# A fused attention and mixture-of-experts kernel: a rebuilt opening, spread activation loads, two weight low halves on VectorE and a moved routing step

## The chip, the core and the metric

The kernel runs on one core of a Trainium2 chip. That core has TensorE (matrix products into PSUM), VectorE, ScalarE and GpSimd (element work), SyncE (here a queue that issues transfers) and 16 DMA engines. The metric is the device time of one execution in microseconds (us), lower is better. In the views PE is TensorE, DVE is VectorE, ACT is ScalarE, POOL is GpSimd and SP is SyncE.

## The reference

```python
def _attn_ref(q, k, v, g_norm):            # (4, 8, 576, 64) each
    kv = np.einsum('bhsd,bhse->bhde', k, v)
    out = np.einsum('bhsd,bhde->bhse', q, kv)
    rms = np.sqrt(np.mean(out * out, axis=-1, keepdims=True) + 1e-06)
    return (out / rms * g_norm)
def _moe_ref(x, w_gate, w1, w2):           # N=2304, D=512, E=8, F=1024
    P = np.exp(logits - logits.max())      # logits = x @ w_gate
    for _ in range(8):
        P /= P.sum(1, keepdims=True) + 1e-09
        P /= P.sum(0, keepdims=True) + 1e-09
        P *= N / E
    for e in range(E):                     # every token through every expert
        out += P[:, e:e + 1] * (np.maximum(x @ w1[e], 0.0) @ w2[e])
def _moe2_ref(x, expert_emb, tau, w1, w2): # each token through one expert
    logits = xn @ en.T / tau               # xn, en: rows divided by their norms
    expert_idx = np.argmax(logits, axis=1)
    gate_w = softmax(logits)[np.arange(N), expert_idx]
    for e in range(E):
        mask = expert_idx == e
        out[mask] = gate_w[mask, None] * (np.maximum(x[mask] @ w1[e], 0.0) @ w2[e])
```

The last stage's output is the result: attention, then the first mixture, then the second.

## The kernel before

All products are fp32 made of two fp32r parts. A weight or an activation is split into a high half (a cast) and a low half (the rest, `raw - high`), and each product is three matmuls: high by high, high by low, low by high. The split of one 512 KB weight quarter is one `prep(g)`: ScalarE casts the high half `wh` (L158), and the low half `wl` is made either by VectorE in one instruction over 128x1024 (L165, L257) or by GpSimd in two over 128x512 (L163).

The first mixture walks 3 blocks of 768 tokens by 8 experts (step s = 8·block + expert). Its up product uses seven combined products n = 0 to 6 instead of eight (`fill`, L1018): each pairs a combination of weight quarters with one of the activation quarters x11, x21, t2, t3, t4, t1, x22. An activation combination has its own high and low parts, made by `x_split`; for instance `ready_t2` forms `x12-x11` and t2 on VectorE. Each product n has eight columns of work i = 0 to 7 in two loops; `ahead(g)` prepares the weight combination three products ahead (`prep` where it has to be split, `fetch` from a stored copy `w1c`, `w2c` in later blocks), and in the first step (s=0) the table `opening` gives the pieces of attention that are put behind each column. Blocks 1 and 2 have the activations of their four quarters loaded from `xd` by `x_stage` (L300); the down product there is `down` (L1154), whose stored weights `w2c` come on the same SyncE queue.

The opening runs attention for batches 0 to 3, in chunks c = 0 to 4 of up to 128 rows. `att_kv(b, chunks)` accumulates kᵀv (L411), `att_out` multiplies by q (L422), `squares`, `norm_b`, `norm_c` and `scale_rows` (L425 to L439) normalise, `turn` (L446, L447) transposes rows into x. The first `fill` needs x11, which chunks 0 to 2 of batch 0 hold, and the split of w11 (`prep(0)`). Batch 0 comes first, and the others are put between `fill`s.

Element work without a due time is kept in lists (`hooks`: gates, Sinkhorn rows) that advance one entry for each column of the up product in steps s=1 and on; `thooks` are the quarter combinations on GpSimd in that stage.

The second mixture runs each token through one expert: tokens are counted and sorted by matmuls with one-hot matrices (L861 with `B` and `G`), gathered by row by GpSimd's indirect transfers (L1590), and go in blocks of 256 through `f1` (up, L644, then `hh` = relu on ScalarE L648 and `hl` = low half on VectorE L649) and `f2` (down, L664). The gate weight of a token is found from `gate_parts` (L852 to L855): a chain of eight VectorE instructions, three times cast to bf16 and multiply (612 elements a lane), with two subtractions; here called through `q_parts`. Two dynamic blocks follow the fixed ones. The last part goes by blocks of 128 tokens through `single` (L1609 on), where relu gives `hrow`, a transpose on TensorE `hth` and its low half `htl` (L1633).

Of the kernel before, what the change touches and what calls it, by code (L numbers as in the profile page):

```python
# [18 lines left out]
P = 128  # L19
# [25 lines left out]
def tile_linattn_moe_moe(ctx: ExitStack, tc: tile.TileContext, qT, k, v, g2, wg, w1a, w2a, emb, embT, tau, w1b, w2b, out):  # L45
# [246 lines left out]
    def x_stage(blk):  # L292
# [5 lines left out]
        for i, t in enumerate(ts):  # L298
            c = o + i % 2 * HB
            nc.sync.dma_start(t, xd[:, i // 2 * 2:i // 2 * 2 + 2, c:c + HB])  # L300
        return ts
# [235 lines left out]
    for c in range(NSC - 1):  # L537
        load_kv(1, c)
    load_quarter(0, "w11", raws[0, "w11"])
    load_kv(1, NSC - 1)  # L540
# [4 lines left out]
    for c in range(3):  # L545
        load_kv(2, c)
    for name in ("w21", "w22"):
        load_quarter(0, name, raws[0, name])
    for c in range(3, NSC):
        load_kv(2, c)  # L550
    outs = []
    for c in range(NSC):
# [3 lines left out]
        squares(ps, n, c, (junk, x2t)[c % 2])  # L556
        outs.append(ps)
    norm_b(slice(0, NSC))
    norm_c(slice(0, NSC))
    prep(0, nc.gpsimd)  # L560
    for c in range(NSC):
        scale_rows(xs0[c], outs[c], rows_of(c), c)
    att_kv(1, range(NSC - 1))
    for c in range(NSC - 1):
        load_kv(3, c)
# [6 lines left out]
    for c in range(3):  # L572
        first_turn(c)
    for kk in range(2):
        nc.scalar.copy(x_part(0, 0)[:, kk], x11[:, kk])  # L575
        nc.vector.tensor_tensor(x_part(0, 1)[:, kk], x11[:, kk], f32(x_part(0, 0)[:, kk]), ALU.subtract)
    att_kv(1, (NSC - 1,))
# [29 lines left out]
    def open_first():  # L607
# [4 lines left out]
        0: [first_pieces, lambda: att_kv(2, (0,)), lambda: gate_logits(0, 0, 3)],  # L612
        1: [lambda: first_turn(3), lambda: att_kv(2, (1,)), lambda: gate_logits(0, 1, 3)],
        2: [lambda: first_turn(4), lambda: load_kv(3, 4), lambda: stream_turn(1, 0), lambda: gate_logits(0, 2, 3),
            lambda: att_kv(2, (2,)), lambda: prep(2)],
        3: [lambda: stream_turn(1, 1), ready_t2, lambda: att_kv(2, (3, 4)), open_first],
        4: [lambda: x_split("t2", t2), lambda: ahead(0), lambda: gate_logits(3, 3, 6)],
        5: [ready_t3, lambda: gate_logits(3, 4, 6)],
        6: [lambda: gate_logits(3, 5, 6)],
        7: [lambda: att_kv(3, (0,)), lambda: stream_load_q(1)],  # L620
# [403 lines left out]
    def ahead(g):  # L1024
        h = g + 3
        if h < len(seq_of):
            s, n = seq_of[h]
            if s < E or h in plain_at or n >= 7 and not quick(s):
                pool = n in POOL_LOW and (s, n) != (NSTEP - 1, 9) if s < E or not quick(s) and n >= 7 else True
# [199 lines left out]
    n_att = 12  # L1229
# [17 lines left out]
    hooks.extend([sk_max, rest, sk_max1, rest, rest, sk_exp, rest, rest])  # L1247
# [8 lines left out]
    for s in range(NBK * E):  # L1256
# [39 lines left out]
        for n in range(7):  # L1296
# [5 lines left out]
            for i in range(4):  # L1302
# [43 lines left out]
                if i == 1 and g > 0:  # L1346
                    ahead(g)
                if s == 0:
                    for f in opening.get(4 * n + i, ()):
                        f()  # L1350
                if (n, i) in xup:
# [13 lines left out]
        if e == E - 1 and blk + 1 < NBK and not fast:  # L1365
            xq = x_steps(*x_stage(blk + 1))
# [519 lines left out]
```

## Time and profile before

| what | value |
|---|---|
| median of 3 runs | 1792.01 us (1791.96 to 1793.23) |
| the profiled execution, its own time | 1792.93 us |
| span of the trace | 1791.1 us |
| TensorE busy | 1766.2 us (99%), 11494 matmul records |
| VectorE, ScalarE, GpSimd busy | 1244.5 (69%), 849.8 (47%), 1044.6 (58%) us |
| mean granted TensorE clock | 0.998 |

The profiled execution is 0.92 us above the median. The span leaves 1.8 us of its time outside the trace. TensorE is nearly always busy, so the time is the sum of its matmuls, of the time before the first and after the last of them, and of its waits between.

### The profile page before, as it was taken

The page shows a single profiled execution, that of the slowest core. Times are in us where ns is not written, and L with a number is a line of the kernel's source. Part 1 is how long each engine was busy: PE and PEld are TensorE (multiplying, and loading weights), DVE is VectorE, ACT ScalarE, POOL GpSimd, SP SyncE. Part 2 cuts the span into 40 slices and gives each one's busy share as a digit, 9 for nine tenths or more (in the row PEclk, how much of TensorE's full clock was granted, in tenths as well). Part 3 has the DMA queues.
Part 4 walks back from the last instruction along what each step waited for, and adds up shares of the span by engine and source line. Part 5 has one row for each costly group of instructions (what it writes and reads, how often), then busy time and mean ns, then how long its engine had stood idle before and what let it go on. Part 6 is the DMA issues. An engine that isn't in the chain of part 4 may idle for free. (4 is left out here: it accounts for less than half of the span.)

```text
span 1791.1 us, 30992 instructions
## 1 busy us (share of the span) xinstructions
PE 1766.2 (99%) x11494; PEld 1677.6 (94%) x11494; DVE 1244.5 (69%) x2184; ACT 849.8 (47%) x1444; POOL 1044.6 (58%) x867
## 2 busy tenths in 40 slices
PE   7999999999999999999999999999999999999997
PEld 7989889989998999999999999999999998888996
DVE  5946686566657788876456769897567763877665
ACT  4645345444434634544444553554454433556553
POOL 3403379889879655774467566765477432554222
PEclk9999999999999999999999999999999999999999
DMA  9626458779868765556566666566465653588664
GB/s 313 229 59 210 142 207 298 257 262 334 287 232 279 278 221 209 200 190 230 173 222 221 213 228 239 184 218 224 168 214 187 232 203 108 188 315 290 230 232 147
DMA packets 183585, 397.22 MB, mean 222 GB/s; under 512 B 16384, under 2 KB 84480, under 8 KB 183168
## 3 DMA queue, kind: packets, MB, share of 16 engines
q1 hardware_dynamic: 177200, 377.15, 61.2%
q0 software_dynamic: 3840, 12.59, 2.0%
q10 hardware_dynamic: 2384, 5.41, 0.9%
q8 instruction: 92, 1.51, 0.3%
q14 instruction: 69, 0.57, 0.1%
HBM read 314.08 MB, written 81.00 MB: 221 GB/s over the span
## 5 line engine op out<-in xcount | busy, mean ns | idle before, releaser
L1018 PE MATMUL A<-xo,wh 128*128 128x384 f32 x2688 | 689.0, 338 | 0.5 <-ACT xo L575 0.2
L1018 PEld LDWEIGHTS A<-xo,wh 128*128 128x128 f32 x2688 | 482.1, 188 | 3.0 <-DVE u L1006 0.8
L1018 PE MATMUL A<-xo,wl 128*128 128x384 f32 x1344 | 452.1, 336 | 1.4 <-POOL wl L163 1.4
L1154 PE MATMUL A<-wh,d 128*128 128x256 f32 x2520 | 432.2, 276 | 0.2 <-DMA wh<-w2c 0.2
L163 POOL TENSOR_TENSOR wl<-raw,wh 128x512 fp32r<-128x512 f32 x180 | 246.7, 1392 | 289.3 <-ACT wh L158 134.8
L1154 PEld LDWEIGHTS A<-wh,d 128*128 128x128 f32 x2520 | 381.0, 188 | 0.4 <-issue 0.4
L1154 PE MATMUL A<-wl,d 128*128 128x256 f32 x1260 | 348.0, 276 | 0.8 <-DMA wl<-w2c 0.8
L1018 PEld LDWEIGHTS A<-xo,wl 128*128 128x128 f32 x1344 | 252.6, 188 | 2.6 <-POOL wl L163 2.6
L1387 PE MATMUL A<-wh,d 128*128 128x512 f32 x768 | 243.8, 392 | 0.0
L1154 PEld LDWEIGHTS A<-wl,d 128*128 128x128 f32 x1260 | 236.5, 188 | 1.0 <-DMA wl<-w2c 1.0
L1003 DVE SCALAR_TENSOR_TENSOR d<-A,d 128x384 fp32r<-128x384 f32 x228 | 125.9, 553 | 153.7 <-ACT raw L1313 84.1
L163 POOL TENSOR_TENSOR wl<-rb,wh 128x512 fp32r<-128x512 f32 x92 | 129.3, 1426 | 158.6 <-ACT wh L158 158.6
L1387 PEld LDWEIGHTS A<-wh,d 128*128 128x128 f32 x768 | 144.2, 188 | 29.8 <-issue 0.3
L1008 ACT ACTIVATE d<-A 128x384 fp32r<-128x384 f32 x132 | 65.5, 497 | 196.8 <-DVE A L1006 193.8
L1387 PE MATMUL A<-wl,d 128*128 128x512 f32 x384 | 149.5, 389 | 0.0
L1309 ACT COPY qs<-A 128x384 f32<-128x384 f32 x96 | 45.6, 479 | 178.8 <-PE A L1018 175.5
L158 ACT CAST wh<-raw 128x1024 fp32r<-128x1024 f32 x94 | 98.5, 1048 | 14.6 <-DMA raw<-in_w1a_dram 7.3
L257 DVE TENSOR_TENSOR wl<-raw,wh 128x1024 fp32r<-128x1024 f32 x45 | 70.7, 1573 | 35.3 <-ACT wh L256 25.4
L1387 PEld LDWEIGHTS A<-wl,d 128*128 128x128 f32 x384 | 72.2, 188 | 14.0
L1006 DVE TENSOR_TENSOR A<-A,qs 128x384 f32<-128x384 f32 x132 | 73.6, 560 | 16.2 <-PE A L1018 15.9
L158 ACT CAST wh<-rb 128x1024 fp32r<-128x1024 f32 x46 | 48.6, 1056 | 59.8 <-DMA rb<-in_w1a_dram 27.4
L1209 POOL TENSOR_TENSOR d<-qs,d 128x384 fp32r<-128x384 f32 x60 | 66.8, 1143 | 16.9 <-ACT d L1207 16.9
(524 smaller groups left out, 3399.8 us busy)
## 6 DMA issues: line engine op xcount, KB each, us to landing
raw<-in_w1a_dram SPq DMA_DIRECT2D x64, 512.0 KB, 4.7
wh<-w1c SPq DMA_DIRECT2D x64, 512.0 KB, 5.0
wl<-w1c SPq DMA_DIRECT2D x64, 512.0 KB, 6.0
wh<-w2c SPq DMA_DIRECT2D x60, 512.0 KB, 5.3
wl<-w2c SPq DMA_DIRECT2D x60, 512.0 KB, 6.1
raw<-in_w2a_dram SPq DMA_DIRECT2D x51, 512.0 KB, 4.3
raw<-in_w1b_dram SPq DMA_DIRECT2D x48, 512.0 KB, 6.4
raw<-in_w2b_dram SPq DMA_DIRECT2D x48, 512.0 KB, 4.1
```

Source lines behind the costliest of these rows:

```text
L158: nc.scalar.copy(hi, raw)
L163: eng.tensor_tensor(lo[:, c], raw[:, c], f32(hi[:, c]), ALU.subtract)
L257: after_two.append([2, lambda: nc.vector.tensor_tensor(lo, src, f32(hi), ALU.subtract)])
L1003: nc.vector.scalar_tensor_tensor(hl[:, i, :], src, 0.0, f32(hh[:, i, :]), ALU.max, ALU.subtract)
L1006: nc.vector.tensor_tensor(dst, ps, u, ALU.add)
L1008: nc.scalar.activation(hq[a][0][:, i, :], dst, AF.Relu)
L1018: nc.tensor.matmul(ps[:, 0:HB], a[:, fs], bb[:, kk, :], start=(first and j == 0), stop=(j == 5), skip_group_check=True)
L1154: nc.tensor.matmul(o, a[:, f, ts_], bb[:, ds_], start=(m in first and j != 1 and i == 0), stop=(i == 11), skip_group_check=True)
L1209: nc.gpsimd.tensor_tensor(a12[1][:, i], qs[:, i], f32(a12[0][:, i]), ALU.subtract)
L1309: nc.scalar.copy(qs[:, i, :], p)
L1387: nc.tensor.matmul(ys[j], a, bb[:, ds_], start=(m + ff + i == 0), stop=(m == 3 and ff == 1 and i == 2))
```

## The change

It has five parts.

- **Opening.** The load of w11 goes ahead of batch 1's chunks on the SyncE queue, those of batch 2 ahead of w21 and w22. The normalisation of batch 0 is cut into chunks 0 to 2 (`first_norm`, `first_scale`) and 3 to 4, and `prep(0)` stands after the first part. Batch 1's kᵀv is taken in three pieces, with the turns of chunks 0 to 2 between them and the last two chunks behind columns of s=0. The table `opening` is in another order: `ready_t2`, `ready_t3` and their splits stand ahead of `ahead(0)` and `ahead(1)`, which move two columns back, and the low half of `prep(2)` is made by GpSimd instead of VectorE. The entries of `hooks` begin two columns later.
- **Two low halves.** For product 6 of steps 3 and 7 VectorE makes `wl` instead of GpSimd.
- **Activation loads.** The four loads of block 2's activations, 384 KB each, are issued at columns 3 of products 0, 2, 4, 6 of the last expert but one, instead of together after product 6.
- **Routing.** `q_idx` and the first gather stand one `f1` slot later; `q_parts` moves from column 4 of the last fixed `f2` to slot 3 of the first dynamic block's `f1`; one Sinkhorn entry moves by one.
- **Single blocks.** In `single` one weight split (`split_w2(1)`) stands after the first transpose, and the low half of the next block's first W1 quarter after the second.

```diff
@@ x_stage
-        for i, t in enumerate(ts):
+
+        def load(i, t):
             c = o + i % 2 * HB
             nc.sync.dma_start(t, xd[:, i // 2 * 2:i // 2 * 2 + 2, c:c + HB])
-        return ts
+
+        return ts, [lambda i=i, t=t: load(i, t) for i, t in enumerate(ts)]
@@ opening
-    for c in range(NSC - 1):
+    load_quarter(0, "w11", raws[0, "w11"])
+    for c in range(NSC):
         load_kv(1, c)
-    load_quarter(0, "w11", raws[0, "w11"])
-    load_kv(1, NSC - 1)
...
+    def first_norm(c0, c1):
+        for c in range(c0, c1):
+            squares(outs[c], rows_of(c), c, (junk, x2t)[c % 2])
+        norm_b(slice(c0, c1))
+        norm_c(slice(c0, c1))
+
+    def first_scale(c0, c1):
+        for c in range(c0, c1):
+            scale_rows(xs0[c], outs[c], rows_of(c), c)
+
...
-        squares(ps, n, c, (junk, x2t)[c % 2])
         outs.append(ps)
-    norm_b(slice(0, NSC))
-    norm_c(slice(0, NSC))
+    first_norm(0, 3)
     prep(0, nc.gpsimd)
-    for c in range(NSC):
-        scale_rows(xs0[c], outs[c], rows_of(c), c)
-    att_kv(1, range(NSC - 1))
+    first_scale(0, 3)
+    att_kv(1, range(2))
...
     for c in range(3):
         first_turn(c)
+    att_kv(1, (2,))
...
-    att_kv(1, (NSC - 1,))
+    first_norm(3, NSC)
+    first_scale(3, NSC)
...
     opening = {
-        0: [first_pieces, lambda: att_kv(2, (0,)), lambda: gate_logits(0, 0, 3)],
-        1: [lambda: first_turn(3), lambda: att_kv(2, (1,)), lambda: gate_logits(0, 1, 3)],
-        2: [lambda: first_turn(4), lambda: load_kv(3, 4), lambda: stream_turn(1, 0), lambda: gate_logits(0, 2, 3),
-            lambda: att_kv(2, (2,)), lambda: prep(2)],
-        3: [lambda: stream_turn(1, 1), ready_t2, lambda: att_kv(2, (3, 4)), open_first],
-        4: [lambda: x_split("t2", t2), lambda: ahead(0), lambda: gate_logits(3, 3, 6)],
-        5: [ready_t3, lambda: gate_logits(3, 4, 6)],
-        6: [lambda: gate_logits(3, 5, 6)],
-        7: [lambda: att_kv(3, (0,)), lambda: stream_load_q(1)],
+        0: [lambda: att_kv(1, (3,))],
+        1: [lambda: att_kv(1, (4,))],
+        2: [first_pieces, lambda: gate_logits(0, 0, 3), lambda: gate_logits(0, 1, 3)],
+        3: [lambda: att_kv(2, (0,)), lambda: gate_logits(0, 2, 3), lambda: att_kv(2, (1,)), lambda: first_turn(3),
+            lambda: first_turn(4), lambda: load_kv(3, 4), lambda: att_kv(2, (2,)), lambda: att_kv(2, (3, 4)),
+            open_first, lambda: prep(2, nc.gpsimd)],
+        4: [lambda: stream_turn(1, 0), lambda: stream_turn(1, 1), ready_t2],
+        5: [lambda: x_split("t2", t2), lambda: gate_logits(3, 3, 6)],
+        6: [ready_t3, lambda: gate_logits(3, 4, 6), lambda: gate_logits(3, 5, 6), lambda: ahead(0)],
+        7: [lambda: ahead(1), lambda: att_kv(3, (0,)), lambda: stream_load_q(1)],
@@ ahead
-                pool = n in POOL_LOW and (s, n) != (NSTEP - 1, 9) if s < E or not quick(s) and n >= 7 else True
+                pool = n in POOL_LOW and (s, n) not in ((NSTEP - 1, 9), (3, 6), (7, 6)) if s < E or not quick(s) and n >= 7 else True
@@ hooks
-    hooks.extend([sk_max, rest, sk_max1, rest, rest, sk_exp, rest, rest])
+    hooks[:0] = [rest] * 2
+    hooks.extend([sk_max, rest, sk_max1, rest, sk_exp, rest])
@@ steps of the first mixture
+                if fast and e == E - 2 and blk + 1 < NBK and i == 3 and n % 2 == 0:
+                    if n == 0:
+                        staged, staging = x_stage(blk + 1)
+                    staging.pop(0)()
...
         if fast:
-            if e == E - 2 and blk + 1 < NBK:
-                staged = x_stage(blk + 1)
             down(s, blk, e)
@@ single
         split_w2(0)
-        split_w2(1)
         t0 = relu(p0)
         up(p1, 1, 0, 6)
         turn(t0)
+        split_w2(1)
         split_w2(2)
...
-        split_w1(0)
+        low0 = split_w1(0)
         turn(t1)
+        low0()
@@ routing
-        if f == 5:
+        if f == 6:
             q_idx()
             gather(0)
...
-        if f == 4:
-            q_parts()
...
             def slot(f):
                 if f % 2 == 0:
                     split_w2(f // 2)
+                if n == 0 and f == 3:
+                    q_parts()
```

The lines below are each engine's instructions in program order, with the line numbers of the kernel they belong to (those of the changed kernel are some ten to twenty higher).

VectorE at the first dynamic block, before (L852 to L855 is `q_parts`, L649 makes an `hl` for each of the eight columns of `f1`, L165 a weight's low half):

```order
L852 CAST gp_16204<-gr_16203 128x18
L853 TENSOR_TENSOR G_15645<-A_15643,gp_16204 128x18x34
L1602 TENSOR_SCALAR y<-A,iota_i 128x512
L649 SCALAR_TENSOR_TENSOR hl_15670<-A,hh_15669 128x256
L165 TENSOR_TENSOR g3l<-raw_15711,g3h 128x1024
L649 SCALAR_TENSOR_TENSOR hl_15698<-A,hh_15697 128x256
L649 SCALAR_TENSOR_TENSOR hl_15732<-A,hh_15731 128x256
L649 SCALAR_TENSOR_TENSOR hl_15752<-A,hh_15751 128x256
L649 SCALAR_TENSOR_TENSOR hl_15778<-A,hh_15777 128x256
L165 TENSOR_TENSOR g1l<-raw_15713,g1h 128x1024
```

and in the changed kernel:

```order
L165 TENSOR_TENSOR g3l<-raw_15715,g3h 128x1024
L659 SCALAR_TENSOR_TENSOR hl_15702<-A,hh_15701 128x256
L659 SCALAR_TENSOR_TENSOR hl_15736<-A,hh_15735 128x256
L659 SCALAR_TENSOR_TENSOR hl_15756<-A,hh_15755 128x256
L862 CAST gp_16305<-gs 128x18
L863 TENSOR_TENSOR G_15649<-A_15647,gp_16305 128x18x34
L865 TENSOR_TENSOR gr_16304<-gs,gp_16305 128x18
L862 CAST gp_16305<-gr_16304 128x18
L863 TENSOR_TENSOR G_15649<-A_15647,gp_16305 128x18x34
L865 TENSOR_TENSOR gr_16304<-gr_16304,gp_16305 128x18
L862 CAST gp_16305<-gr_16304 128x18
L863 TENSOR_TENSOR G_15649<-A_15647,gp_16305 128x18x34
```

The chain of `q_parts` stood ahead of the block's `hl`s, and now stands behind the fourth of them; the next rows of the changed kernel are the fifth `hl` and `g1l`.

TensorE in the opening, before (L411 is kᵀv, L446 a turn, L1018 the first product of the mixture; `qs`, `u`, `kv` hold batch 1's chunks):

```order
L411 MATMUL A<-qs 128x128 x4
L411 MATMUL A<-u_153,qs 128x128 x4
L411 MATMUL A<-u_153 128x128 x4
L411 MATMUL A<-kv 128x128 x4
L446 MATMUL M<-ident,xs_148 128x128 x12
L411 MATMUL A<-kv 128x128 x4
L1018 MATMUL A<-xo,wh 128x384 x2
L1018 MATMUL A<-xo,wl 128x384
L1018 MATMUL A<-xo,wh 128x384 x2
L1018 MATMUL A<-xo,wl 128x384
L422 MATMUL M<-ax,q_147 64x128 x4
L422 MATMUL M<-ax,q_147 128x128 x4
```

and in the changed kernel, where L413, L448 and L1028 are the same three:

```order
L413 MATMUL A<-qs 128x128 x4
L413 MATMUL A<-u_153,qs 128x128 x4
L448 MATMUL M<-ident,xs_148 128x128 x12
L413 MATMUL A<-u_153 128x128 x4
L1028 MATMUL A<-xo,wh 128x384 x2
L1028 MATMUL A<-xo,wl 128x384
L1028 MATMUL A<-xo,wh 128x384 x2
L1028 MATMUL A<-xo,wl 128x384
L413 MATMUL A<-kv 128x128 x4
L1028 MATMUL A<-xo,wh 128x384 x2
L1028 MATMUL A<-xo,wl 128x384
L1028 MATMUL A<-xo,wh 128x384 x2
```

The turns of batch 0 stand two chunks of batch 1 earlier, and its last two chunks stand behind the first columns of the product.

GpSimd in the opening, before (L163 is a low half, L263 a weight combination, L290 an activation's low half):

```order
L290 TENSOR_TENSOR xo<-x_145,xo 128x384 x2
L163 TENSOR_TENSOR wl<-raw,wh 128x512 x2
L263 TENSOR_TENSOR raw<-raw 128x512 x2
L163 TENSOR_TENSOR wl<-raw,wh 128x512 x2
L263 TENSOR_TENSOR raw<-raw 128x512 x2
```

and in the changed kernel:

```order
L290 TENSOR_TENSOR xo<-x_145,xo 128x384 x2
L163 TENSOR_TENSOR wl<-raw,wh 128x512 x4
L263 TENSOR_TENSOR raw<-raw 128x512 x2
L163 TENSOR_TENSOR wl<-raw,wh 128x512 x2
L263 TENSOR_TENSOR raw<-raw 128x512 x2
```

Two more low halves stand ahead of the combination.

## Rows read from the trace of the kernel before

**Rows 1.** Page, part 1: busy time, share of the span and instructions.

```profile
PE 1766.2 (99%) x11494; PEld 1677.6 (94%) x11494; DVE 1244.5 (69%) x2184; ACT 849.8 (47%) x1444; POOL 1044.6 (58%) x867
```

**Rows 2.** Waits of TensorE: line, what it waited for, total us, times, longest.

```profile
PE M L411 <- DMA rb<-in_v_dram: 4.5, 1, 4.5
PE M L446 <- ACT x L447: 2.0, 1, 2.0
PE A L1018 <- POOL wl L163: 1.4, 3, 0.8
PE M L411 <- DMA kv<-in_v_dram: 1.4, 1, 1.4
PE A L422 <- ACT qxa L418: 0.9, 1, 0.9
PE A L1154 <- DMA wl<-w2c: 0.8, 1, 0.8
PE M L861 <- DVE B L1566: 0.5, 1, 0.5
PE A L1643 <- DVE htl L1633: 0.3, 1, 0.3
```

**Rows 3.** Timelines of ScalarE, VectorE and TensorE in the opening; start, duration, idle before.

```profile
17.36 0.60 ACT L425 ACTIVATE xj<-A 128x512 f32<-128x512 f32 x1 [0.30 <-PE A L422]
23.78 1.04 ACT L158 CAST wh<-raw 128x1024 fp32r<-128x1024 f32 x1 [3.73 <-DMA raw<-in_w1a_dram]
...
21.49 1.89 DVE L439 TENSOR_TENSOR xs<-A,ri 128x512 f32<-128x512 f32 x3
...
21.50 1.13 PE L411 MATMUL A<-kv 128*128 128x128 f32 x8 [0.28 <-DMA kv<-in_v_dram]
...
27.44 1.04 PE L1018 MATMUL A<-xo,wh 128*128 128x384 f32 x2 [0.24 <-ACT xo L575]
```

**Rows 4.** Timeline of GpSimd in the opening's second half.

```profile
40.52 3.56 POOL L263 TENSOR_TENSOR raw<-raw 128x512 f32<-128x512 f32 x2 [2.36 <-DVE raw L215]
```

**Rows 5.** Timelines of GpSimd and TensorE at the low half of step 3.

```profile
291.04 2.86 POOL L163 TENSOR_TENSOR wl<-raw,wh 128x512 fp32r<-128x512 f32 x2
...
293.95 0.44 PE L1018 MATMUL A<-xo,wl 128*128 128x384 f32 x1 [0.76 <-POOL wl L163]
```

**Rows 6.** Timelines of SyncE's DMA queue and TensorE around block 1's last expert.

```profile
955.54 0.98 SPq L300 DMA_DIRECT2D qxa<-xd  x2
...
967.54 0.35 PE L1154 MATMUL A<-wh,d 128*128 128x256 f32 x1 [0.21 <-DMA wh<-w2c]
968.74 0.39 PE L1154 MATMUL A<-wl,d 128*128 128x256 f32 x1 [0.84 <-DMA wl<-w2c]
```

**Rows 7.** Timelines of VectorE, GpSimd and TensorE around the first dynamic block.

```profile
1578.46 1.41 DVE L649 SCALAR_TENSOR_TENSOR hl<-A,hh 128x256 fp32r<-128x256 f32 x4
1580.30 2.06 DVE L165 TENSOR_TENSOR g1l<-raw,g1h 128x1024 fp32r<-128x1024 f32 x1 [0.43 <-ACT g1h L158]
...
1578.86 2.42 POOL L165 TENSOR_TENSOR g0l<-raw,g0h 128x1024 fp32r<-128x1024 f32 x1 [2.63 <-ACT g0h L158]
1581.84 2.78 POOL L165 TENSOR_TENSOR g2l<-raw,g2h 128x1024 fp32r<-128x1024 f32 x1 [0.56 <-ACT g2h L158]
1584.58 2.40 POOL L165 TENSOR_TENSOR w11l<-raw,w11h 128x1024 fp32r<-128x1024 f32 x1
...
1583.38 0.39 PE L664 MATMUL A<-g1l,hh 128*128 128x512 f32 x1
```

**Rows 8.** Tile `gp` (ns min/median/max), then timelines of VectorE and GpSimd at 1434 us.

```profile
L852 DVE CAST gp<-gr x6: 173/180/1156, 1350.4 to 1573.3; 128x12 bf16<-128x12 f32 x4, 128x18 bf16<-128x18 f32 x2
L853 DVE TENSOR_TENSOR G<-A,gp x3: 796/796/798, 1571.2 to 1573.5; 128x612 bf16<-128x612 bf16 x3
...
1434.95 1.16 DVE L853 TENSOR_TENSOR pG<-pA,gp 128x24 bf16<-128x24 f32 x1
...
1434.77 2.59 POOL L163 TENSOR_TENSOR wl<-rb,wh 128x512 fp32r<-128x512 f32 x2
```

More of the change, by code (lines that the diff above doesn't have):

```diff
@@ L544, in tile_linattn_moe_moe @@
     att_kv(0)
-    for c in range(3):
+    for c in range(NSC):
         load_kv(2, c)
@@ L548, in tile_linattn_moe_moe @@
         load_quarter(0, name, raws[0, name])
-    for c in range(3, NSC):
-        load_kv(2, c)
     outs = []
+    def first_norm(c0, c1):
[6 more added lines that the diff above has]
+            scale_rows(xs0[c], outs[c], rows_of(c), c)
     for c in range(NSC):
@@ L555, in tile_linattn_moe_moe @@
         att_out(ps, 0, q01[0][:, :, c * P:c * P + n], n)
-        squares(ps, n, c, (junk, x2t)[c % 2])
         outs.append(ps)
-    norm_b(slice(0, NSC))
-    norm_c(slice(0, NSC))
+    first_norm(0, 3)
     prep(0, nc.gpsimd)
-    for c in range(NSC):
-        scale_rows(xs0[c], outs[c], rows_of(c), c)
-    att_kv(1, range(NSC - 1))
-    for c in range(NSC - 1):
-        load_kv(3, c)
+    first_scale(0, 3)
+    att_kv(1, range(2))
     for i in (0, 2):
@@ L573, in tile_linattn_moe_moe @@
         first_turn(c)
+    att_kv(1, (2,))
+    for c in range(NSC - 1):
+        load_kv(3, c)
     for kk in range(2):
@@ L1226, in scores @@
         return (lambda: logits(t, t + 1)) if whole else rest
-    n_att = 12
+    n_att = 14
     late_x = {6: lambda: x_split("t4", x21), 8: lambda: x_split("t1", x11, nc.gpsimd),
@@ L1345, in tile_linattn_moe_moe @@
                         tails.pop(0)()
-                if i == 1 and g > 0:
+                if i == 1 and g > 1:
                     ahead(g)
@@ L1365, in tile_linattn_moe_moe @@
         if e == E - 1 and blk + 1 < NBK and not fast:
-            xq = x_steps(*x_stage(blk + 1))
+            ts, loads = x_stage(blk + 1)
+            for f in loads:
+                f()
+            xq = x_steps(*ts)
         if e == 2 and blk == 0:
@@ L1801, in split_w1 @@
             def split_w1(kk):
+                if kk == 0:
+                    hi, lo = w1n[kk] = [get(places["w10"][0], [P, 1024], F32R, "w10" + c) for c in "hl"]
+                    nc.scalar.copy(hi, raw1[kk])
+                    return lambda: nc.vector.tensor_tensor(lo, raw1[kk], f32(hi), ALU.subtract)
                 pool = kk == 2
```

## The prediction

> **What bounds the kernel now.** I read the page's busy shares first. TensorE is busy for 1766.2 of the 1791.1 us span [rows 1], so the other 24.9 us are all that a change without fewer matmuls can reach, and the instructions of both kernels in program order show the same matmuls in both. Next I read what TensorE waited for [rows 2]. The reader is to see that the waits are few and short. The first is 4.5 us for the first load, then 1.4 and 0.9 us in the attention of batch 0, and the change touches none of these. The last matmul is done about 10.7 us before the span's end, and nothing there is touched either (24.9 less the waits, which come to 14.2, 11.8 of them in these rows). That leaves 14.2 - 4.5 - 1.4 - 0.9 = 7.4 us that this change could take away at the very best. The time can't fall below 1792.0 - 7.4 = 1784.6 us, while a new wait has no such bound. Then I read timelines around each place that the change edits.
>
> **The opening.** Within reach here are the 2.0 us in which a turn waits for ScalarE's copy [rows 2], and 0.28 and 0.24 us ahead of a chunk and of the first product [rows 3]: 2.5 in all. ScalarE stood 3.73 us waiting for w11, until 23.78 [rows 3], and its copies are queued behind that cast. With w11 ahead of five pairs of loads, it lands well before its cast is due. The next thing is then the normalisation of chunks 0 to 2. The first scaling starts at 21.49 and takes 1.89/3 = 0.63 us [rows 3], so the first rows are ready at 22.12. Squaring a chunk takes 0.60 us on ScalarE with 0.30 of waiting ahead of it [rows 3], so with two chunks fewer the scaling comes some 1.8 to 2.1 us earlier (the square roots behind are over 24 columns instead of 40), and the first rows are ready at about 20.05. The turns, copies and splits behind them keep their length, and as ScalarE no longer stands between the second and the third turn for 2.0 us, the first product comes at about 23.45 in place of 27.44 [rows 3]. Two of these four microseconds are only exchanged, since two chunks of batch 1 (1.1 us for each, as the one at 21.50) now come behind the first product. The lead is about 2.0 us.
>
> The lead is then partly given back. GpSimd now makes the low half of w21's combination (two instructions, 2.86 us at 291.04 [rows 5]) ahead of the L263 combination that started at 40.52 and took 3.56 [rows 4], and this group now runs while VectorE forms x12-x11, t2 and their low half. The products behind them wait for a combination of PSUM on ScalarE whose cast waits for that group. I put the first wait at 0.35 us (what is left of one GpSimd half of 1.4 when VectorE comes an instruction of 1.1 later) and the second at 0.8 (about half of one L263 instruction, 1.8): estimates, since no row shows this order. That is 1.15 off the lead of 2.0 to 2.2. So I take **-1.0 us**, with -2.2 (nothing given back) and +1.0 (each microsecond beyond these is lost whole, TensorE being busy) as bounds.
>
> **The two low halves on VectorE.** TensorE waited 0.76 us at 293.95 for `wl`, which GpSimd made from 291.04 to 293.90 [rows 5], although its cast was long done: it was queued behind the combinations on GpSimd. Step 7 has the two other waits of the three, 1.4 in all [rows 2]; with the pipeline's refill, about 0.2 for each, the three come to 1.9. VectorE takes one instruction instead, 1.1 us when nothing holds it and 2.06 when GpSimd does (both from `g1l`, below). If the longer one makes the next activation late by the difference of 1.0, half of the gain is gone. I take **-1.6** (-1.9 to -1.0).
>
> **The activation loads.** Two loads of 384 KB were issued in 955.54 to 956.5 and two more right behind them, all ahead of the weights that TensorE then waited for, 0.21 us at 967.54 and 0.84 at 968.74 [rows 6]; with the refill these come to 1.46. Issued over seven products, they are through before. I take **-1.45** (-1.46 to -1.0).
>
> **Small moves.** TensorE waited 0.5 us for `B`, on which the index sum depends [rows 2]; one slot later it is there. But the gather starts later too, and whether it is then waited for, no row says: between -0.7 and 0, and I take **-0.3**. In `single` the waits for `htl` come to 0.3 [rows 2]. They go if VectorE reaches `htl` a weight split earlier, but ScalarE now makes `hrow` behind one more cast (about 1 us) close to its due time, so between -0.3 and +0.5, and I take **+0.15**. The Sinkhorn entry and the hooks' shift lie in steps where VectorE and GpSimd have room: 0.
>
> **The routing chain decides.** `q_parts` is eight instructions on VectorE. Before, it ran from 1571.0 to 1574.3, with GpSimd idle, and cost nothing: the next `hl` waited for ScalarE behind it anyway. Each of its three multiplications takes 0.80 us free and a cast 0.18 [rows 8]; three of the one, and five small ones at about 0.18, make 3.3. Now it is queued behind the fourth `hl`, and behind it are the fifth `hl`, `g1l` and the last three. The second to the fifth `hl` start at 1578.46 and take 1.41, 0.35 each [rows 7], so the fourth is done at about 1579.5. TensorE wants `g1l` at 1583.38 [rows 7]. If nothing disturbs the chain: 1579.5 + 3.3 + 0.35 + 1.1 (an undisturbed low half) = 1584.25, or a stall of 0.9.
>
> But GpSimd makes `g0l`, `g2l` and `w11l` in 1578.86 to 1586.98, with a gap of 0.56 [rows 7], and the rows show that the two engines hold each other up. `g1l` took 2.06 there: `g0l` ended at 1578.86 + 2.42 = 1581.28, and `g1l` 1.08 after that [rows 7], so it waited, and its own work is 1.1. The same chain over a tiny tile shows it better: a cast takes 0.18 us as a rule and 1.156 at worst, a multiplication of 24 columns 1.16 [rows 8]. That multiplication, at 1434.95, ended at 1436.1, when the first of the two GpSimd instructions that began at 1434.77 was done (2.59/2 = 1.3). Each instruction of the chain can thus wait out one of GpSimd's, here 2.4 us long. Going through it in turns: the first cast waits to 1581.3, a multiplication follows to 1582.15, `g2l` holds the next up to 1584.6, `w11l` to 1587.0, and the rest (two multiplications and small ones) ends at 1588.85, `hl` at 1589.2 and `g1l` at 1590.3. That is a stall of 7.0; if VectorE gets in before `w11l`, it is 7.0 less `w11l`'s 2.4, 4.6. I take **+6.5**, near the upper end since in the rows each one of the two waits out the other (0.9 to 7.0).
>
> On this place bears a rule of the Trainium skill (SBUF — State Buffer, "Who interferes with whom"): VectorE and GpSimd share a pair of ports as an exclusive lock, held for the whole instruction, and a VectorE instruction with two SBUF inputs contends with a GpSimd instruction that reads SBUF. The trace agrees: the `hl`s, with one input in PSUM, took 0.35 each beside `g0l`, and `g1l`, with two in SBUF, 2.06 [rows 7]. By it the stall would be 4.6 to 7.0 and not 0.9.
>
> **The sum.** -1.0 - 1.6 - 1.45 - 0.3 + 0.15 + 6.5 = +2.3 us. The profiled execution took 1792.93, so a like one would take 1795.2. It lay 0.92 above the median of 1792.01, and against that the forecast is **1794.3 us**. About 0.2%, 3.6 us, is what a measurement of this kernel can tell from no change, so this counts as the same.
>
> **The rivals.**
> - *The chain doesn't wait for GpSimd* (faster). Then the stall is 0.9, the sum -3.3 and the time 1788.7; with the opening's whole lead kept (-2.2) it is -4.5, 1787.5. For it speaks that before, GpSimd had a gap of 0.56 us there, and that small casts mostly take 0.18. Against it: the rows at 1434 us, where the same chain was held. It counts as faster from an opening of -1.3 on, some half of this case. Chance 0.28: 0.16 faster, 0.12 the same.
> - *The opening's lead is lost* (slower). Without the opening the sum is +3.3, so from +0.3 there on the change is slower. One microsecond more of waiting for the L263 group, behind which the PSUM combination stands, is enough: an opening of +1.0 gives 1796.3, and with a stall of 7.0 1796.8. For it speaks that GpSimd was idle there before and now isn't; against it that 2.0 us of lead have to go first. Chance 0.26.
> - *VectorE gets in between* `g2l` *and* `w11l`: a stall of 4.6, a sum of +0.4, 1792.4, the same. Chance 0.14.
> - The forecast itself: 0.32, the same.
>
> The two cases of both signs are not unlikely, so the likeliest one's own range is 1793 to 1795.6. The range of 8 in 10 goes from 1787.8 (most of the first rival) to 1797.3 (the second with both ends of its bounds). Chances: faster 0.16, the same 0.58 (0.12 + 0.14 + 0.32), slower 0.26.
>
> **What would show it.** The opening: the first product at about 23.5, and new waits of TensorE between 40 and 55 us. The low halves and loads: no wait at 293.95, 542, 543 and 968. The chain: one wait of TensorE of 4 to 7 us for `g1l` or the fifth `hl` in the first dynamic block, with the casts of `q_parts` drawn out over a microsecond while GpSimd works. If that wait is about 1 us or missing, the forecast is wrong on the side of faster; if the waits of the opening pass 2 us, on the side of slower.

## The result and the profile after

The changed kernel took 1804.02 us (median of 6 runs, 1803.26 to 1804.62) against 1792.62 of the kernel before on the same chip (6 runs, 1790.31 to 1794.40): a ratio of 1.0066, with a 95% interval of 1.0055 to 1.0077. It is 11.4 us slower. The forecast was 1794.3, with a range of 1787.8 to 1797.3: the measured time lies above it. The span of the changed kernel's trace is 1802.5 us.

The first line of the page of the changed kernel, and then TensorE's waits (line, what was waited for, total us, times, longest), beside [rows 1, 2]:

```profile
PE 1771.4 (98%) x11494; PEld 1679.6 (93%) x11494; DVE 1250.7 (69%) x2189; ACT 850.7 (47%) x1445; POOL 1046.1 (58%) x865
```

```profile
PE A L674 <- DVE g1l L165: 6.9, 2, 6.6
PE M L413 <- DMA rb<-in_v_dram: 4.6, 1, 4.6
PE A L1028 <- DVE u L1016: 1.6, 4, 0.7
PE M L413 <- DMA kv<-in_v_dram: 1.0, 1, 1.0
PE A L654 <- DVE w11l L165: 0.9, 2, 0.5
PE A L1645 <- ACT hrow L1639: 0.6, 2, 0.3
PE M L448 <- ACT rb L489: 0.5, 1, 0.5
PE M L457 <- ACT xj L449: 0.5, 1, 0.5
```

Two things are to be seen. All the waits that the change aimed at have gone: `wl` from GpSimd, `wl` from `w2c`, `B`, `htl`. In their place stand others: `u`, `w11l`, `hrow`, and one of 6.6 us for `g1l`. And TensorE's busy time has grown, from 1766.2 [rows 1] to 1771.4, though its matmuls are the same 11494. A sum of waits can't explain that part.

Since the matmuls are the same, the two traces can be laid side by side matmul by matmul. The difference in start (after minus before) grows or falls where something happens:

| stretch (us in the kernel before) | the difference goes from, to | step |
|---|---|---|
| opening, to 172 | 0 to +0.35 | +0.35 |
| 172 to 292 (at 231) | +0.35 to +0.15 | -0.2 |
| step 3 (292 to 297) | +0.15 to +0.03 | -0.1 |
| step 7 (536 to 546) | +0.03 to +1.0 | +0.95 |
| block 1's last expert (967 to 969) | +1.0 to -0.6 | -1.6 |
| 969 to 1583 (+0.5 at 1375, -0.25 from the index at 1553 on, +0.5 at 1577) | -0.6 to +0.1 | +0.7 |
| `g1l` of the first dynamic block (1583.4) | +0.1 to +6.95 | +6.8 |
| the matmuls right behind it (1583.4 to 1586.1) | +6.95 to +9.4 | +2.45 |
| the 128-token blocks (1599 to 1643) | +9.4 to +11.5 | +2.1 |

Each step is measured against one execution of the kernel before. Kernels that have its code in a stretch still differ from it there: by -1.9 to +2.3 us in the opening, by -0.8 to -1.4 at 967 to 969 and by +0.1 to +0.65 at 1577 to 1583. A step there is the change's only as far as it goes beyond these.

The biggest step is the wait. VectorE's timeline in the changed kernel (start, duration) shows the chain (L862 to L865) behind three `hl`s, and the two rows of TensorE that follow the wait, a timeline of their own:

```profile
1578.58 1.08 DVE L659 SCALAR_TENSOR_TENSOR hl<-A,hh 128x256 fp32r<-128x256 f32 x3
1579.58 1.85 DVE L862 CAST gp<-gs 128x18 bf16<-128x18 f32 x1
1581.46 0.80 DVE L863 TENSOR_TENSOR G<-A,gp 128x612 bf16<-128x612 bf16 x1
1582.18 2.36 DVE L865 TENSOR_TENSOR gr<-gs,gp 128x18 f32<-128x18 f32 x1
1584.57 2.27 DVE L862 CAST gp<-gr 128x18 bf16<-128x18 f32 x1
1586.88 0.80 DVE L863 TENSOR_TENSOR G<-A,gp 128x612 bf16<-128x612 bf16 x1
...
1589.06 1.21 DVE L165 TENSOR_TENSOR g1l<-raw,g1h 128x1024 fp32r<-128x1024 f32 x1
```

```profile
1590.33 0.80 PE L674 MATMUL A<-g1l,hh 128*128 128x512 f32 x1 [6.64 <-DVE g1l L165]
1590.92 0.63 PE L674 MATMUL A<-g1h,hl 128*128 128x512 f32 x1
```

GpSimd's timeline beside it:

```profile
1578.99 2.40 POOL L165 TENSOR_TENSOR g0l<-raw,g0h 128x1024 fp32r<-128x1024 f32 x1 [6.01 <-ACT g0h L158]
1581.98 2.53 POOL L165 TENSOR_TENSOR g2l<-raw,g2h 128x1024 fp32r<-128x1024 f32 x1 [0.58 <-ACT g2h L158]
1584.46 2.35 POOL L165 TENSOR_TENSOR w11l<-raw,w11h 128x1024 fp32r<-128x1024 f32 x1
```

A cast of 18 columns took 1.85 and then 2.27 us, a subtraction of 18 columns 2.36; between them a multiplication of 612 columns took its 0.80. The three that were drawn out ended at 1581.43, 1584.54 and 1586.84, each 0.03 to 0.04 us after one of GpSimd's three. `g1l` ended at 1590.27, where the prediction's queue had put 1590.3. What the prediction didn't have is in the second fence: these matmuls of 512 columns took 0.80 and 0.63 us, where the same ones took 0.39 before [rows 7]. The windows of the changed kernel (length; busy time of PE, PEld, DVE, ACT and POOL; then granted clock, DMA share, GB/s) say why:

```profile
1582.00:1590.00 8.00, 1.68 (x8) 1.06 (x6) 7.86 (x9) 4.16 (x5) 4.81 (x2) 0.91 0.61 245
1590.00:1594.00 4.00, 3.67 (x23) 2.96 (x24) 2.06 (x8) 0.00 (x0) 0.00 (x0) 0.50 0.67 216
1594.00:1598.00 4.00, 4.00 (x18) 3.27 (x17) 3.64 (x4) 0.59 (x1) 0.00 (x0) 0.82 0.97 342
1598.00:1602.00 4.00, 4.00 (x19) 3.29 (x19) 0.90 (x2) 0.00 (x0) 0.99 (x1) 1.00 0.73 294
```

In 1590 to 1594 the granted clock is 0.50, the lower of TensorE's two levels (1.2 instead of 2.4 GHz); by 1598 it is back at 1.00. It fell while the engine stood (the 0.91 of the window ahead), in a wait of 6.6 us.

### The profile page after: what moved, and what is told of

The parts are those of the page before. It is cut to its first block, busy times and chain, and to the rows that moved or that the text cites. A ratio compares the mean times of both kernels' runs of the same rounds, so it can differ in the third digit from the quotient of the medians.

```text
span 1802.5 us, 30992 instructions
## 1 busy us (share of the span) xinstructions
PE 1771.4 (98%) x11494; PEld 1679.6 (93%) x11494; DVE 1250.7 (69%) x2189; ACT 850.7 (47%) x1445; POOL 1046.1 (58%) x865
## 5 line engine op out<-in xcount | busy, mean ns | idle before, releaser
L1028 PE MATMUL A<-xo,wh 128*128 128x384 f32 x2688 | 689.6, 338 | 2.6 <-DVE u L1016 1.6
L1028 PEld LDWEIGHTS A<-xo,wh 128*128 128x128 f32 x2688 | 481.6, 188 | 7.2 <-DVE u L1016 3.1
L1028 PE MATMUL A<-xo,wl 128*128 128x384 f32 x1344 | 451.6, 336 | 0.0
L163 POOL TENSOR_TENSOR wl<-raw,wh 128x512 fp32r<-128x512 f32 x178 | 246.2, 1405 | 290.4 <-ACT wh L158 170.8
L1028 PEld LDWEIGHTS A<-xo,wl 128*128 128x128 f32 x1344 | 252.6, 188 | 0.0
L163 POOL TENSOR_TENSOR wl<-rb,wh 128x512 fp32r<-128x512 f32 x92 | 128.6, 1419 | 158.1 <-ACT wh L158 158.1
L1018 ACT ACTIVATE d<-A 128x384 fp32r<-128x384 f32 x132 | 65.5, 498 | 192.5 <-DVE A L1016 188.7
L257 DVE TENSOR_TENSOR wl<-raw,wh 128x1024 fp32r<-128x1024 f32 x47 | 74.8, 1594 | 35.6 <-ACT wh L256 26.6
```

The lines of the kernel that those rows point to most:

```text
L163: eng.tensor_tensor(lo[:, c], raw[:, c], f32(hi[:, c]), ALU.subtract)
L257: after_two.append([2, lambda: nc.vector.tensor_tensor(lo, src, f32(hi), ALU.subtract)])
L1018: nc.scalar.activation(hq[a][0][:, i, :], dst, AF.Relu)
L1028: nc.tensor.matmul(ps[:, 0:HB], a[:, fs], bb[:, kk, :], start=(first and j == 0), stop=(j == 5), skip_group_check=True)
```

## The experiments

Each was run beside the kernel before on the same chip. Where 0.2% is too coarse, the place is read in the trace, at the same matmuls.

**The chain back in its old place.** All other parts of the change stay.

```diff
@@ the last fixed f2
+        if f == 4:
+            q_parts()
@@ the first dynamic block's slot
-                if n == 0 and f == 3:
-                    q_parts()
```

> The changed kernel with the routing chain back in its old place, all other parts kept. Theory 1 (the wait and the clock behind it are one cause): TensorE's wait of 6.9 us at the fifth column goes, and so do the 2.4 us that the lower clock level took behind it, so about 1794.7 us, 9.4 less than the changed kernel, and the granted clock is 1.00 from 1582 to 1598. Theory 2 (the clock fell for another reason, such as the time since the start): only 6.9 us go, about 1797.1, and the clock falls as before somewhere near 1590.

It took 1794.76 us, a ratio of 1.0007 (0.9998 to 1.0017): 1.2 above the kernel before beside it, where the changed kernel was 11.4 above. At the same matmuls nothing is left of the 6.8 and 2.45 us at `g1l`. TensorE was busy for all of 1582 to 1598 at a clock of 1.00. Theory 1: the wait and the low clock go together.

**The chain moved alone**, on the kernel before.

```diff
-        if f == 4:
-            q_parts()
...
+                if n == 0 and f == 3:
+                    q_parts()
```

> The kernel before with nothing but the routing chain moved. Theory 1: a wait of about 6.9 us for g1l and 2.4 us at the lower clock level, about 9.3 us slower than before. Theory 2: 6.9 us slower, with no fall of the clock behind it. Rival 3 (the wait needs the other parts, for instance later weight halves): less than 5 us.

It took 1801.57 us, a ratio of 1.0042 (1.0025 to 1.0059), which is 8.0 us slower by the runs (4.5 to 10.6). At the same matmuls the step is 6.9 for `g1l` and 2.5 behind it, with a clock of 0.50 in 1590 to 1594. Nothing else of the change is needed for it.

**GpSimd idle beside the chain.** In the changed kernel VectorE makes the three low halves of that block.

```diff
-                w2t[i] = split(raw2[i], f"w2{i}", nc.gpsimd if n == 0 and i % 2 else None)
+                w2t[i] = split(raw2[i], f"w2{i}", None)
...
-                w1t[:] = [split(raw1[kk], f"w1{kk}", nc.gpsimd if kk == 1 else None) for kk in range(KC)]
+                w1t[:] = [split(raw1[kk], f"w1{kk}", nc.gpsimd if kk == 1 and n > 0 else None) for kk in range(KC)]
```

> The changed kernel with the three low halves of the first dynamic block (g0l, g2l, w11l) made by VectorE instead of GpSimd, so GpSimd is idle while the chain runs. Theory 1 (each of the chain's instructions waits out one of GpSimd's): although VectorE has 1.1 us more ahead of g1l, the chain takes 3.3 us instead of 9.2, g1l is done at about 1585.5 and TensorE waits about 2.1 us; if a wait that short leaves the clock alone, 7.2 us less than the changed kernel. Rival (the queue on VectorE alone is the cause): g1l comes 1.1 us later than in the changed kernel, the wait is 8 us.

It took 1797.01 us, a ratio of 1.0020 (1.0010 to 1.0029), 3.4 above the kernel before. At the same matmuls the step is 2.0 for `g1l` and 0.1 behind it, together 7.1 less than in the changed kernel. The timelines of VectorE and of TensorE in this kernel:

```profile
1580.51 0.17 DVE L862 CAST gp<-gs 128x18 bf16<-128x18 f32 x1
1580.71 0.80 DVE L863 TENSOR_TENSOR G<-A,gp 128x612 bf16<-128x612 bf16 x1
1581.42 0.17 DVE L865 TENSOR_TENSOR gr<-gs,gp 128x18 f32<-128x18 f32 x1
1581.63 0.18 DVE L862 CAST gp<-gr 128x18 bf16<-128x18 f32 x1
...
1584.03 1.21 DVE L165 TENSOR_TENSOR g1l<-raw,g1h 128x1024 fp32r<-128x1024 f32 x1
```

```profile
1585.30 0.50 PE L674 MATMUL A<-g1l,hh 128*128 128x512 f32 x1 [1.83 <-DVE g1l L165]
```

The same instructions take 0.17 and 0.18 us now; the chain took 3.3 us instead of 9.2, although VectorE had one low half more ahead of it. What stretched them was GpSimd's work and not the queue. The wait of 1.83 us left the clock at 1.00.

**One of GpSimd's three taken away.** Only `w11l` goes to VectorE:

```diff
-                w1t[:] = [split(raw1[kk], f"w1{kk}", nc.gpsimd if kk == 1 else None) for kk in range(KC)]
+                w1t[:] = [split(raw1[kk], f"w1{kk}", nc.gpsimd if kk == 1 and n > 0 else None) for kk in range(KC)]
```

> The changed kernel with w11's low half alone taken from GpSimd and made by VectorE behind g1l; g0l and g2l stay on GpSimd. Theory 1: the chain waits out g0l and g2l but not w11l, so g1l comes 2.3 us earlier than in the changed kernel and TensorE waits 4.6 us (the prediction's third case). If the clock falls by the length of the wait, the lower level costs some of the 2.4 us behind it, else nothing: 2.3 to 4.7 us less than the changed kernel, 1799.3 to 1801.7. Rival: g1l's place in VectorE's queue decides, no difference.

It took 1801.63 us, a ratio of 1.0049 (1.0034 to 1.0065), 9.5 above the kernel before. Timelines of VectorE and TensorE, then the windows, of this kernel:

```profile
1579.04 1.85 DVE L862 CAST gp<-gs 128x18 bf16<-128x18 f32 x1
...
1581.64 2.36 DVE L865 TENSOR_TENSOR gr<-gs,gp 128x18 f32<-128x18 f32 x1
1584.04 0.18 DVE L862 CAST gp<-gr 128x18 bf16<-128x18 f32 x1
```

```profile
1587.70 0.79 PE L674 MATMUL A<-g1l,hh 128*128 128x512 f32 x1 [4.58 <-DVE g1l L165]
```

```profile
1582.00:1590.00 8.00, 3.42 (x22) 2.36 (x22) 6.51 (x11) 3.71 (x4) 1.97 (x1) 0.70 0.71 259
1590.00:1594.00 4.00, 4.00 (x21) 3.31 (x19) 3.42 (x6) 0.03 (x1) 0.00 (x0) 0.74 0.96 360
1594.00:1598.00 4.00, 4.00 (x19) 3.29 (x18) 2.96 (x4) 0.55 (x1) 0.76 (x1) 1.00 0.88 334
```

Two stretched instructions instead of three, one for each of GpSimd's, and a wait of 4.58 us, which is the prediction's third case to the tenth. The clock still fell. At the same matmuls the step is 4.7 for `g1l` and 2.1 behind it, together 2.4 less than in the changed kernel. So the lower level cost 0.1 or nothing behind 1.83 us, 2.1 behind 4.58 and 2.45 behind 6.64. The length of the wait doesn't set that cost by itself: by the clocks of the windows (0.70 and 0.74 here, 0.91, 0.50 and 0.82 in the changed kernel) the clock fell at about 1585.2 and 1588.6, 2.1 and 4.9 us into the two waits, and was back at about 1592.1 and 1595.4. TensorE worked at the lower level for 4.4 and 5.1 us, and somewhat less than half of that was lost.

**The 128-token blocks alone.**

```diff
         split_w2(0)
-        split_w2(1)
         t0 = relu(p0)
         up(p1, 1, 0, 6)
         turn(t0)
+        split_w2(1)
         split_w2(2)
...
-        split_w1(0)
+        low0 = split_w1(0)
         turn(t1)
+        low0()
...
```

> The kernel before with the change in the 128-token blocks alone. Theory 1 (what the two traces show at the same matmuls): the wait for htl goes (-0.45 us a block), a wait for hrow of 0.5 takes its place, and the next block's first columns wait 0.7 to 0.9 us for w12l and w11l, in each of two blocks: 1.5 to 2.1 us slower, hardly more than a run can tell, but read off the same matmuls in the trace. Theory 2 (these waits come from the delay and the low clock ahead of them): no difference, within 0.3 us.

It took 1796.16 us, a ratio of 1.0013 (1.0004 to 1.0023). At the same matmuls the difference goes from +0.1 at 1598 to +1.9 behind 1643, a step of 1.8: theory 1.

**Its first half alone.**

```diff
-        split_w2(1)
         t0 = relu(p0)
         up(p1, 1, 0, 6)
         turn(t0)
+        split_w2(1)
```

> The kernel before with one half of the change in the 128-token blocks: the W2 split moved behind the first transpose, the next block's first W1 low half left in its place. Theory 1: this half brings the gain at htl (-0.45 us a block) and the wait for hrow (+0.5), and the waits for w12l and w11l (0.9 us a block) belong to the other half: about 0 at the end. Rival: everything behind moves by one split in any case, 1.5 us or more slower.

It took 1792.59 us, a ratio of 1.0000 (0.9991 to 1.0009): no difference that the runs can tell. In the trace the difference goes from -2.4 ahead of the blocks to -1.55 behind them, so this half costs 0.45 us a block, between the two expectations. The waits of this kernel show both at once:

```profile
PE A L1629 <- ACT hrow L1623: 0.6, 2, 0.3
PE A L1643 <- DVE htl L1633: 0.6, 2, 0.3
```

The new wait for `hrow` comes, and the one for `htl` doesn't go (0.3 once in the kernel before [rows 2], twice here). With the other half too, `htl`'s wait is gone and `w11l`'s is there.

**The opening alone.** The kernel before with the whole of the diff's opening (its loads, `first_norm`, `first_scale` and table) and the lines that go with it:

```diff
-    n_att = 12
+    n_att = 14
...
-    hooks.extend([sk_max, rest, sk_max1, rest, rest, sk_exp, rest, rest])
+    hooks[:0] = [rest] * 2
+    hooks.extend([sk_max, rest, sk_max1, rest, sk_exp, rest])
...
-                if i == 1 and g > 0:
+                if i == 1 and g > 1:
                     ahead(g)
```

> The kernel before with the rebuilt opening alone. Theory 1 (what both traces show at the same matmuls): the first product comes 4 us earlier and TensorE waits some 0.7 us less up to 200 us, but the products come no earlier from 165 us on: 0 to +0.4 us, no difference in the time. Rival (the prediction's step): -1.0 us, kept to the end.

It took 1792.15 us, a ratio of 0.9997 (0.9987 to 1.0007). The first product comes at 23.28; from 164 to 967 us the products come 0.3 to 0.6 later than in the kernel before. Theory 1. (Its ten runs lie within 1.5 us of each other, on which more below.)

**The two low halves alone.**

```diff
-                pool = n in POOL_LOW and (s, n) != (NSTEP - 1, 9) if s < E or not quick(s) and n >= 7 else True
+                pool = n in POOL_LOW and (s, n) not in ((NSTEP - 1, 9), (3, 6), (7, 6)) if s < E or not quick(s) and n >= 7 else True
```

> The kernel before with the two low halves on VectorE alone. Theory 1 (the wait moves from wl to VectorE's own next work, since the low half takes 1.9 us beside GpSimd and stands ahead of it): at 296 us -0.5 us, at 546 us +0.4 to +0.9 more, in all 0 to +0.5. Rival (the prediction's step): both waits for wl go and nothing takes their place, -1.6.

It took 1793.68 us, a ratio of 1.0007 (0.9997 to 1.0016). At the same matmuls step 3 gives -0.15 and step 7 +0.95, +0.8 in all: the wait moves, as theory 1 says, and costs more than it says. At step 3 the 1.1 us gained at `wl` are given back but for 0.15, so -0.5 there was too much.

**The activation loads alone.**

```diff
...
+                if fast and e == E - 2 and blk + 1 < NBK and i == 3 and n % 2 == 0:
+                    if n == 0:
+                        staged, staging = x_stage(blk + 1)
+                    staging.pop(0)()
...
-            if e == E - 2 and blk + 1 < NBK:
-                staged = x_stage(blk + 1)
```

> The kernel before with the spread activation loads alone. Both the prediction's step and the traces say that the waits for w2c at 967 to 969 us go: -1.4 to -1.6 us at the same matmul behind them. Rival: something else late behind it takes part of it back, -0.5 or less at the end.

It took 1791.88 us, a ratio of 0.9997 (0.9987 to 1.0006). In the trace the difference falls by 1.6 us at 967 to 969, and 1.5 are left at the end. But these waits are not the same in every execution. In six other kernels the loads stand as in the kernel before, and over the same matmuls these came 0.8 to 1.4 us earlier than its profile did. For two of them the list of waits has none for `w2c` there. A third, the kernel with the chain moved alone, shows half of the longer one:

```profile
PE A L1154 <- DMA wl<-w2c: 0.4, 1, 0.4
```

So the spread loads gain between 0.2 and 1.6 us, 0.7 in the middle one of the seven. The step is right in its cause, its size is that of one execution, and it is smaller than what the runs can tell.

**The index one slot later, alone.**

```diff
-        if f == 5:
+        if f == 6:
             q_idx()
             gather(0)
```

> The kernel before with the index sum and the first gather one slot later, nothing else. Theory 1: the wait for B goes (-0.7 to -1.3 us at 1554 us), and later waits for the chain of index, gather and turn give it back by 1577 us: 0 at the end. Rival (the prediction's step): -0.3 to -0.7 is kept.

It took 1792.93 us, a ratio of 1.0003 (0.9994 to 1.0013). The difference goes from +1.1 at 1550 to -0.3 at 1554 and +0.9 from 1561 to 1577: of the 1.4 us gained 0.25 is kept so far, and the same 0.25 in the other four kernels with the index moved. From 1577 to 1583 the difference rises to +1.4. The seven kernels that have both index and chain in their old places are later there too, by 0.1 to 0.65 us, so that part isn't shown to be the index's.

**What is left that could gain**, with the new opening and without: the loads as above and the low half of step 3 only.

```diff
-                pool = n in POOL_LOW and (s, n) != (NSTEP - 1, 9) if s < E or not quick(s) and n >= 7 else True
+                pool = n in POOL_LOW and (s, n) not in ((NSTEP - 1, 9), (3, 6)) if s < E or not quick(s) and n >= 7 else True
```

> The kernel before with the rebuilt opening, the spread loads and one low half on VectorE, that of step 3, and nothing else of the change. If the parts add up (0 for the opening, -1.5 for the loads, -0.5 for the low half): about 2 us faster than the kernel before, 1790.4, with runs within 2 us of each other as in the opening alone. Rival: a low clock in the opening that the kernel before has in some executions makes the difference between the openings, -2.5 to -3.

> The same without the rebuilt opening: the kernel before with the spread loads and the low half of step 3 on VectorE. If the parts add up, -2 us, 1790.4. Rival (the old opening falls to the lower clock level in some executions): the same best time, but runs spread over 4 to 6 us as those of the kernel before.

They took 1791.51 us, a ratio of 0.9998 (0.9989 to 1.0007), and 1792.07, a ratio of 0.9991 (0.9982 to 1.0001). Neither can be told from the kernel before, and the 2 us by which the parts should add up can't be seen in the runs. The sizes in that sum were too large: the low half of step 3 gains 0.1 in both traces, and the loads 0.7 in the middle and not 1.5. The runs spread over 2.2 us with the new opening and 3.8 with the old. No version is shown to beat the kernel before.

## Why the prediction was wrong

**The chain** (+6.5 forecast). Measured +6.8, by the mechanism given: one instruction of VectorE waits out one of GpSimd's. With none of GpSimd's, two of them and all three beside it, TensorE waited 1.8, 4.6 and 6.6 us. This step held, and the first rival (no wait for GpSimd) is out.

**The sum** is the step that failed first: it counted a wait of TensorE at its own length. Behind a wait of 4.6 us and more the granted clock was 0.50, and the matmuls that follow cost 2.1 to 2.5 us more. No term and no rival had this, and the range couldn't either, since its upper end took the chain at its own 7.0. (That end, 1797.3, is said to be the second rival with both ends of its bounds, which the prediction itself adds up to 1796.8. All upper bounds together give +6.5 or 1798.5, still 5.5 below the measured time.) The lower level alone doesn't make the miss: two more terms failed by about 2 us each, the 128-token blocks and the low halves.

**The 128-token blocks** (+0.15, bounds -0.3 to +0.5). Measured +1.8 alone and +2.1 in the changed kernel: mis-sized, and outside its bounds. The wait for `hrow` came as feared. What was late next wasn't followed up: the work that was put off lands where the next block's weights are split. Timelines of TensorE, VectorE and GpSimd in the changed kernel:

```profile
1609.94 0.66 PE L1645 MATMUL A<-ident,hrow 128*128 128x128 f32 x4 [0.31 <-ACT hrow L1639]
1617.70 0.39 PE L654 MATMUL A<-xh,w11l 128*128 128x256 f32 x1 [0.46 <-DVE w11l L165]
```

```profile
1613.08 1.22 DVE L165 TENSOR_TENSOR w13l<-raw,w13h 128x1024 fp32r<-128x1024 f32 x1
1615.42 2.23 DVE L165 TENSOR_TENSOR w11l<-raw,w11h 128x1024 fp32r<-128x1024 f32 x1
```

```profile
1613.29 3.27 POOL L165 TENSOR_TENSOR w12l<-raw,w12h 128x1024 fp32r<-128x1024 f32 x1 [4.08 <-ACT w12h L158]
```

`w13l` of VectorE and `w12l` of GpSimd meet, `w12l` takes 3.27 us, and `w11l` behind it 2.23, until TensorE waits.

**The two low halves** (-1.6, bounds -1.9 to -1.0). Measured +0.8 alone and +0.85 in the changed kernel. TensorE's waits for `wl` went, but the price of the low half was taken as 1.1 us where nothing holds it, and only half of the gain was put at risk. Timelines of VectorE and TensorE at step 7 in the changed kernel:

```profile
533.63 1.90 DVE L257 TENSOR_TENSOR wl<-raw,wh 128x1024 fp32r<-128x1024 f32 x1 [0.95 <-ACT wh L256]
535.45 0.55 DVE L1329 TENSOR_TENSOR u<-A,qs 128x384 f32<-128x384 f32 x1
```

```profile
541.82 0.59 PE L1028 MATMUL A<-xo,wh 128*128 128x384 f32 x2 [0.29 <-DVE u L1016]
543.85 0.62 PE L1028 MATMUL A<-xo,wh 128*128 128x384 f32 x2 [0.75 <-DVE u L1016]
546.68 0.62 PE L1028 MATMUL A<-xo,wh 128*128 128x384 f32 x2 [0.26 <-DVE u L1016]
```

The low half takes 1.90 us beside GpSimd, and everything on VectorE behind it (the sums `u` first) is late by 1 us, for which TensorE waits three times, 1.3 in all. That is the upper one of the two prices that the prediction had, with all of its cost on the path. At step 3 it is the same on a smaller scale: the products behind are late by what `u` is late, and 0.1 of the gain is left.

**The opening** (-1.0). The first product came at 23.33 (forecast 23.45), and the lead was lost as the second rival said, but elsewhere: not at the L263 group at 40 to 55 us. Timeline of TensorE in the changed kernel:

```profile
23.33 0.44 PE L1028 MATMUL A<-xo,wh 128*128 128x384 f32 x1 [0.43 <-ACT xo L583]
...
65.89 0.59 PE L1028 MATMUL A<-xo,wh 128*128 128x384 f32 x2 [0.25 <-DVE u L1329]
72.47 1.06 PE L457 MATMUL M<-wgs,xj 128*128 128x8 f32 x8 [0.47 <-ACT xj L449]
...
81.93 0.66 PE L448 MATMUL M<-ident,ax 128*128 128x128 f32 x4 [0.47 <-ACT rb L489]
```

By 165 us TensorE's gaps behind its first matmul came to 4.4 us instead of 5.1, but the same products, turns and gate matmuls took 1.0 us longer between their starts, in the new order, and the first load came 0.1 later. These together are the +0.35 that is left. That the new order itself makes the matmuls slower is read from the starts alone, and wasn't tried apart.

The term has a second fault: the 2.0 us that a turn waits for ScalarE [rows 2] were read off one execution. In the profile of the kernel with the first half of the blocks' change, whose opening is the old one, w11 was there sooner (its cast starts at 20.97 and not 23.78 [rows 3]), and the same wait is

```profile
PE M L446 <- ACT x L447: 0.2, 1, 0.2
```

There the product of 163.7 us comes at 161.8, ahead of all six profiles with the new opening (164.0 to 164.4).

**The loads** (-1.45) gave -1.6 against the same execution that the prediction read, and about half as much against the middle of seven. **The index** (-0.3) gave -0.25 up to 1577 us; what comes behind it was not shown to be its doing.

In sum, forecast against measured: chain 6.5 and 6.8, low clock 0 and 2.45, blocks 0.15 and 2.1, low halves -1.6 and +0.85, opening -1.0 and +0.35, loads -1.45 and -1.6, index -0.3 and -0.25. To these come +0.8 that no term had (-0.2 at 231 us, +0.5 at 1375 and +0.5 at 1577), which some profiles of kernels with the same code there show and others don't. The sums are +2.3 and +11.5.

## What to carry to other kernels

Where TensorE is nearly always busy, ask for each new wait not only how long it is but what the clock does behind it. Small VectorE instructions in a dependent chain are priced by what GpSimd does beside them: eight instructions worth 3.3 us cost 9.2, because three of them each waited out one of 2.4 us. Put such a chain where GpSimd is idle, as it stood before. And a low half moved from a late engine to a nearly full one moves the wait with it, unless what is queued behind it has that much room. Before a wait is counted as a gain, see whether another execution of the same code has it too: the 2.0 us at the turn were 0.2 in one, and the 0.8 at `w2c` were 0.5 or less in six others.

## What the runs showed of the hardware

*The clock falls in the old opening too, in some executions.* Windows of the kernel with the two low halves alone, whose opening is that of the kernel before:

```profile
26.00:28.00 2.00, 1.62 (x9) 1.17 (x8) 1.03 (x2) 1.90 (x5) 0.94 (x2) 0.85 1.03 383
28.00:30.00 2.00, 2.00 (x8) 1.56 (x8) 0.00 (x0) 0.46 (x1) 0.00 (x0) 0.50 1.05 383
30.00:32.00 2.00, 2.00 (x15) 1.83 (x14) 0.00 (x0) 0.77 (x3) 0.00 (x0) 0.80 1.05 386
```

TensorE had waited 1.73 us for a copy at 24.96. Of the eight profiles with the old opening, five had such a stretch at 0.50 within the first 34 us (this one again at 42 us); of the six with the new one, none. The product that stands at 163.7 us in the kernel before came between 161.8 and 166.0 in the eight, and between 164.0 and 164.4 in the six. The runs agree: ten of the new opening alone spread over 1.5 us (1791.71 to 1793.16), the 31 of the kernel before beside them over 6.0 (1789.43 to 1795.47). So the new opening moves no median, but narrows the spread. The clock isn't all of that spread: the 161.8 and the 163.7 both come from profiles without a fall, with 0.2 and 2.0 us of waiting at the turn. Why the clock falls in some executions behind waits of 1.7 to 2.0 us and not in others (the profile of the kernel before has a wait of 1.96 us and no fall) stays open: four of the five falls stand behind such a wait at 25 us, the fifth at 14 us behind shorter ones. The Trainium skill (TensorE: Matmul & The Clock Gate, "What's actually happening") says that the lower level is the default that activity releases; the two levels and the fall behind idle time agree with it (0.50 behind 4.58 and 6.64 us).

*Issue order between the two engines.* In the rows of the changed kernel three of the chain's eight instructions waited, one for each of GpSimd's. Ahead of `g2l`, where GpSimd had stood idle for 0.58 us, a multiplication got through at its own 0.80; between `g2l` and `w11l`, which stood ready, only the subtraction did. The rule that the prediction cites from the Trainium skill (SBUF — State Buffer, "Who interferes with whom") names instructions with two SBUF inputs, and casts in certain modes. No row shows in which mode the chain's casts ran, but a cast with one input of 18 columns waited too, 1.85 and 2.27 us.
